# A spectral mixing layer with a snake feed-forward: the first batch's stage on pairs of PSUM banks, its filter in three groups, with copies moved to GpSimd

## The chip, the core and the metric

The kernel runs on one core of a Trainium2 chip. The metric is the device time of one launch in microseconds. Names of engines in the profile: PE is TensorE's matmul and PEld its weight load, DVE is VectorE, ACT is ScalarE, POOL is GpSimd, SP is SyncE, which only issues DMAs here.

## The reference

```python
X = np.fft.rfft(x, axis=1)                     # x: 8 x 3008 x 256
y = np.fft.irfft(X * (filt_r + 1j * filt_i), n=3008, axis=1)
h = y.reshape(24064, 256) @ w_in               # 256 x 2048
g = h + np.sin(alpha * h) ** 2 / (alpha + 1e-9)
out = g @ w_out                                # 2048 x 256, float32
```

## The kernel before, in words

The sequence of 3008 points is taken as 47 x 64, so that both transforms become matmuls with small tables: a first stage over 47, a turn of the data, a stage over 64 in 24 classes of frequencies, a product with the filter, and the same back. Weights are folded: `w_in` is multiplied by alpha, `w_out` by -1/(2 alpha), and the loop then needs only a cosine.

Most of the time is a loop of 48 chunks of up to 512 columns: `hidden` (the first product, line 601, cosine on ACT at L605, one operation on DVE at L606) and `project` (the second product, L621). The transforms of batches 1 to 7 are put between its steps by a list of places (`put`). PE is nearly always busy there.

Before the loop can begin stands the head: the transform of batch 0, done whole in SBUF, and the loads and folding of weights. The order on every engine is the order of the program text (a manual schedule). The head's steps, with the names that the change and the prediction touch:

- Loads. SP loads the first quarter of x in two halves (into `cos_all`). POOL's queue loads the other three quarters, the table `d_t`, an identity `id16`, and then the filter: for each of two groups of 12 classes, two DMAs of the real part, two of the imaginary part, and one for `e_t` (L364, L368). At most eight of POOL's DMAs are under way: each further one waits on POOL for the landing of the one eight before it. `split_alpha` on POOL splits alpha in three bf16 parts between those issues. SP's `w_in` DMAs wait for the landing of the real part of group 1; small tables and `w_out` are queued behind them on SP.
- Stage one. `warm_pe` runs matmuls on a zero tile, so as to keep PE busy. `cast_x0` casts the first quarter of x in two halves on DVE; between them DVE takes the reciprocal of alpha on 16 partitions (L455). 16 matmuls `pa` (L459), each into a PSUM bank of its own out of the pools `hps` (4 banks) and `fps` (2), evacuated on DVE and ACT in turn into `t1_0` (L185 and L187, the helper `evac`).
- `spread_alpha` (L353, L355) broadcasts alpha over partitions by matmuls and copies by ACT, one bank at a time, twice early and twice at the head's end. `inverse_table` (L426, L428) makes `e1_0` from `d_t`.
- `turn` (L473) turns blocks of 32 on DVE: four to get `t2_0`, and two of twice the size (`turn_back`) at the end.
- `other_half` completes the filter on 128 partitions: a copy of the real part to partitions 64 to 127 (L187) and a negation of the imaginary part to partitions 0 to 63 (L445), both on DVE, per group of 12.
- 12 blocks of 4 classes and half of the channels: `forward_0` (PE `pb` L491, ACT L495), `product_0` (DVE, L501, real and imaginary part in one instruction), `inverse_0` (PE `pc` L513, ACT L185).
- `reciprocals` turns 1/alpha to 128 partitions through PE. Then 12 warming matmuls and `last_0` (PE `pd` L403), which give the first columns of `y`, on which `hidden` works.
- `weights_in` and `weights_out` on POOL (L542, L574) fold alpha in. The first waits for the last product.

Of the kernel before, what the change touches and what calls it, by code (L numbers as in the profile page):

```python
# [9 lines left out]
FP16 = mybir.dt.float16  # L10
# [12 lines left out]
NR = 2 * N1  # L23
# [48 lines left out]
def kernel(  # L72
# [31 lines left out]
    def pool(name, bufs, space=None):  # L104
        kw = {} if space is None else {"space": space}
        return ctx.enter_context(tc.tile_pool(name=name, bufs=bufs, **kw))
# [4 lines left out]
    xfpool = pool("xf", 3)  # L111
    ppool = pool("pp", 7)
    xspool = pool("xs", 3)
# [4 lines left out]
    fps = pool("fps", 2, PSUM)  # L118
    hps = pool("hps", 4, PSUM)
    ops = pool("ops", 2, PSUM)  # L120
# [203 lines left out]
    al, rest, rec = [w2_cols[0:16, 256 * i:256 * i + 256].bitcast(FP32) for i in range(3)]  # L324
# [23 lines left out]
    def spread_alpha(i):  # L348

        ps = hps.tile([128, 4, 128], FP32, name=f"al_bc_{i}", tag="h")  # L350
        for a in range(4):
            for k, part in enumerate(parts):
                nc.tensor.matmul(out=ps[:, a, :], lhsT=one[:, 4 * i + a:4 * i + a + 1].to_broadcast([128, 128]),  # L353
                                 rhs=part, start=(k == 0), stop=(k == 2))
        nc.scalar.copy(out=alpha[:, i // 2, 512 * (i % 2):512 * (i % 2) + 512], in_=ps.rearrange("p a b -> p (a b)"))  # L355

    for g in range(2):
        gs = slice(12 * g, 12 * g + 12)
        for k, filt in enumerate((filt_r, filt_i)):
            for q in range(2):  # L360
                if (g, k, q) == (0, 1, 1):
                    split_alpha()
                off, step = ((12 * g) * C, C) if q == 0 else ((N1 - 12 * g) * C, -C)
                marks["filt", g, k] = nc.gpsimd.dma_start(  # L364
                    out=f_t[k][64 * k + 32 * q:64 * k + 32 * q + 32, gs, :],
                    in_=bass.AP(tensor=filt.tensor, offset=filt.offset + off,
                                ap=[[N1 * C, 32], [step, 12], [1, C]]))
        nc.gpsimd.dma_start(out=e_t[:, gs, :], in_=e_dram.ap()[:, gs])  # L368

# [23 lines left out]
    def last_0(n0, n, own=fps, tag="f", spread=False):  # L393

        for cb in range(2):
            made = []

            def one(i, cb=cb, made=made):

                if i == 0:  # L400
                    ps = own.tile([128, 512], FP32, name=f"pd_0_{n0}_{cb}", tag=tag)
                    made.append(ps[:, 0:n * NR].rearrange("p (a r) -> p a r", r=NR))
                nc.tensor.matmul(out=made[0][:, i, :], lhsT=t4_cols[:, n0 + i, :, cb], rhs=wi0_t,  # L403
                                 start=True, stop=True)
                if i == n - 1:
                    evac(y[:, cb, 0, n0:n0 + n, :], made[0], cb == 0)

            for i in range(n):
                if spread:
                    between.append(lambda i=i, one=one: one(i))  # L410
                else:
                    one(i)

    def reciprocals():

        ps = ops.tile([128, 512], FP32, name="ps_rec", tag="o")
        nc.tensor.transpose(out=ps[:, 0:16], in_=rec, identity=id32)
        nc.vector.tensor_scalar(out=rec_t, in0=ps[:, 0:16], scalar1=-0.5, scalar2=None, op0=ALU.mult)

    def inverse_table(g):  # L420

        gs = slice(8 * g, 8 * g + 8)
        ps = ops.tile([128, 8, 128], FP16, name=f"pse_{g}", tag="o")
        for i in range(8):
            for a in range(2):
                nc.tensor.transpose(out=ps[64 * a:64 * a + 64, i, :],  # L426
                                    in_=d_t[:, 8 * g + i, 64 - 64 * a:128 - 64 * a], identity=id16)
        nc.scalar.mul(e1_0[:, gs, :], ps, -0.125)  # L428

    warmed = []  # L430

    def warm_pe(n):

        warmed.append(n)
        ps = hps.tile([128, 512], FP32, name=f"warm_{len(warmed)}", tag="h")
        for i in range(n):
            nc.tensor.matmul(out=ps, lhsT=idle[:, 0:128], rhs=idle[:, 0:512], start=True, stop=True)  # L437

    def other_half(g, k, on_act):

        gs = slice(12 * g, 12 * g + 12)
        if k == 0:
            evac(f_t[0][64:128, gs, :], f_t[0][0:64, gs, :], on_act)
        else:
            nc.vector.tensor_scalar(out=f_t[1][0:64, gs, :], in0=f_t[1][64:128, gs, :],  # L445
                                    scalar1=-1.0, scalar2=None, op0=ALU.mult)
# [8 lines left out]
    nc.vector.reciprocal(out=rec, in_=al)  # L455
    for i in range(16):
        own, tag = (fps, "f") if i % 3 == 2 else (hps, "h")
        ps = own.tile([128, 512], FP32, name=f"pa_0_{i}", tag=tag)
        nc.tensor.matmul(out=ps, lhsT=wf0_t[0:NR], rhs=x0[i // 4][:, 2 * (i % 4):2 * (i % 4) + 2, :],  # L459
                         start=True, stop=True)  # L460
        evac(t1_0[:, 2 * i:2 * i + 2], ps.rearrange("p (n k c) -> p n c k", n=2, k=2), i % 2)
        if i == 1:
            warm_pe(3)
            cast_x0(1)
        if i < 15 and i % 4 == 3:
            warm_pe((2, 2, 2, 1)[i // 4])
    spread_alpha(0)
    spread_alpha(1)
    warm_pe((2, 2, 2, 1)[3])
# [10 lines left out]
    for i in range(4):  # L480
        turn(t2_0[i // 2][:, :, 32 * (i % 2):32 * (i % 2) + 32], t1_0[:, :, 32 * i:32 * i + 32])
        if i > 1:
            other_half(0, i - 2, False)
    blocks = [(hc, w) for hc in range(2) for w in range(3)] + [(0, 3), (1, 3), (0, 4), (0, 5), (1, 4), (1, 5)]
    xf0, p0 = {}, {}

    def forward_0(i):
        hc, w = blocks[i]
        ps = hps.tile([128, 4, 128], FP32, name=f"pb_0_{i}", tag="h")
        for j in range(4):  # L490
            nc.tensor.matmul(out=ps[:, j, :], lhsT=d_t[:, 4 * w + j, :],  # L491
                             rhs=t2_0[hc][:, 4 * w + j], start=True, stop=True)
        own, tag = (xspool, "xs") if i % 2 else (xfpool, "xf")
        xf0[i] = own.tile([128, 4, 128], FP16, name=f"xf_0_{i}", tag=tag)
        nc.scalar.copy(out=xf0[i].rearrange("p s (k c) -> p s k c", k=2),  # L495
                       in_=ps.rearrange("p s (c k) -> p s k c", k=2))

    def product_0(i):
        hc, w = blocks[i]
        p0[i] = xpool.tile([128, 2, 4, 128], FP16, name=f"p_0_{i}", tag="x")  # L500
        marks["products"] = nc.vector.tensor_tensor(  # L501
            out=p0[i].rearrange("p f s (k c) -> p f s k c", k=2),
            in0=xf0[i].rearrange("p s (k c) -> p s k c", k=2)[:, None].to_broadcast([128, 2, 4, 2, 64]),
            in1=filt_t[:, :, 4 * w:4 * w + 4].rearrange("p f s (k c) -> p f s k c", k=2)[..., 64 * hc:64 * hc + 64],
            op=ALU.mult)

    def inverse_0(i):
        hc, w = blocks[i]
        ps = fps.tile([128, 4, 128], FP32, name=f"pc_0_{i}", tag="f")
        for j in range(4):  # L510
            s = 4 * w + j
            for k in range(2):
                nc.tensor.matmul(out=ps[:, j, :], rhs=p0[i][:, k, j, :],  # L513
                                 lhsT=e_t[:, s, :] if k == 0 else e1_0[:, s, :],
                                 start=(k == 0), stop=(k == 1))
        evac(g_0[hc][:, 4 * w:4 * w + 4], ps.rearrange("p s (k c) -> p s c k", k=2), not (i in ()))
# [4 lines left out]
    for g in range(6):  # L521
# [5 lines left out]
        if g == 0:  # L527
            after(ins, marks["filt", 1, 0])
# [19 lines left out]
    [inverse_table(g) for g in range(2)]  # L548
    for i in range(6):
        forward_0(i)  # L550
        if i % 3 == 2:
            if i == 2: inverse_table(2)
            warm_pe((4, 0)[i // 3])
    for i in range(13):
        for e in {5: [(1,0,False)],6: [(1,1,False)]}.get(i, ()):
            other_half(*e)
        if i < 12:
            product_0(i)
        if i == 11:
            reciprocals()  # L560
        if i > 0:
            inverse_0(i - 1)
        if i + 6 < 12:
            forward_0(i + 6)
        if i == 12:
            turn_back(0)
    turn_back(1)

# [8 lines left out]
    spread_alpha(2)  # L577
    spread_alpha(3)
# [6 lines left out]
    last_0(4, 2, hps, "h")  # L585
# [113 lines left out]
    for n0, n, at in ((6, 5, 1.5), (11, 4, 11), (15, 4, 13), (19, 4, 15.5), (23, 4, 17), (27, 5, 19)):  # L699
        put(at, last_0, n0, n, fps, "f", True)  # L700
# [91 lines left out]
```

## Time and profile before

| | |
|---|---|
| median of three runs | 776.99 us (776.43 to 777.83) |
| profiled execution, its own time | 779.76 us |
| its span, first to last instruction | 778.0 us |
| mean granted TensorE clock | 0.997 |
| first `hidden` matmul (chain) | 38.70 us |

The profiled execution is one run with the hardware profiler on; its own time is a little above that of the runs without it. The page gives busy times by engine (part 1) and the chain of work that ended last (part 4). The chain of waits lists the same chain in order of time: start in us, length, engine, tile and line. A timeline lists instructions of an engine in order, merged (x2 is two of them), with the idle time before and what ended it. A view of busy times by stretch adds PE's granted clock, where 1.00 is full speed.

### The profile page before, as it was taken

To read this page: it belongs to the slowest core of one execution; us is meant where nothing else is said; L and a number is where in the kernel's file an instruction comes from. 1 tells how busy PE (TensorE), PEld (TensorE's weight loads), DVE (VectorE), ACT (ScalarE), POOL (GpSimd) and SP (SyncE) were. 2 spreads that over 40 slices of the span, in tenths; PEclk is the share of its full clock that TensorE was granted. 3 is DMA by queue.
4 is the path that set the end of the run, shared out by engine and by line. 5 is a ranking of instruction groups with operands and counts; after the bars stand their busy time and mean duration, and the time that the engine had idled before them with its cause. 6 is when DMAs were issued, how large, how long until landed. Compare 5 with 4: busy or idle time off the path is not lost.

```text
span 778.0 us, 17230 instructions
## 1 busy us (share of the span) xinstructions
PE 764.5 (98%) x6039; PEld 517.0 (66%) x6039; DVE 658.0 (85%) x1174; ACT 610.4 (78%) x1204; POOL 370.4 (48%) x649
## 2 busy tenths in 40 slices
PE   7999999999999999999999999999999999999997
PEld 3757766666666666666666666766666666766665
DVE  6986998999988888898889988898888888787773
ACT  5798888898878877888878787788778787777762
POOL 6355555634555655455464647554454645430000
PEclk9999999999999999999999999999999999999999
DMA  9955578864765428644474536864254322511112
GB/s 223 267 108 160 119 181 242 220 137 124 187 165 133 124 58 219 154 108 127 107 194 121 139 95 145 198 152 120 72 145 110 87 70 56 135 46 34 37 41 56
DMA packets 81518, 101.49 MB, mean 130 GB/s; under 512 B 18884, under 2 KB 60864, under 8 KB 81431
## 3 DMA queue, kind: packets, MB, share of 16 engines
q0 software_dynamic: 27440, 47.29, 26.1%
q1 hardware_dynamic: 53434, 52.79, 25.4%
q8 instruction: 47, 0.77, 0.4%
q10 hardware_dynamic: 557, 0.31, 0.2%
q14 instruction: 40, 0.33, 0.1%
HBM read 56.15 MB, written 46.66 MB: 132 GB/s over the span
## 4 chain that ended last, share of the span: by engine, by line
PE 91%; DVE 5%; ACT 1%; issue 1%; DMA 1%; ACTq 0%; DVEq 0%
PE po L621 40%; PE ph L601 40%; DVE v L606 3%; PE pd L316 2%; PE pb L243 2%; PE pa L222 2%; PE pc L293 1%; ACT cos_all L605 1%; PE pc L513 1%; DMA w<-in_moe_alpha_dram 1%; PE warm L437 1%; PE pb L491 1%; PE pa L459 1%; PE pa L206 0%; PE pd L403 0%
## 5 line engine op out<-in xcount | busy, mean ns | idle before, releaser
L606 DVE SCALAR_TENSOR_TENSOR v<-cos_all,ph 128x512 f16<-128x512 f32 (+1 forms) x768 | 482.5, 671 | 99.2 <-ACT cos_all L605 95.7
L605 ACT ACTIVATE cos_all<-ph 128x512 f32<-128x512 f32 (+1 forms) x768 | 413.9, 600 | 101.8 <-PE ph L601 98.5
L665 POOL DMA_DIRECT2D out_dram<-o x530 | 291.7, 557 | 244.1 <-ACT o L630 215.3
L621 PE MATMUL po<-w,v 128*128 128x256 f16 x3008 | 389.9, 273 | 0.9 <-DVE v L606 0.9
L601 PE MATMUL ph<-y,w 128*128 128x512 f16 (+1 forms) x1536 | 389.1, 375 | 1.3 <-DVE v L606 1.1
L621 PEld LDWEIGHTS <-v 128*128 128x128 f16 x3008 | 289.9, 98 | 85.9 <-DVE v L606 1.5
L601 PEld LDWEIGHTS <-w 128*128 128x128 f16 x1536 | 143.1, 98 | 114.0 <-issue 19.1
L630 ACT COPY o<-po 128x512 f32<-128x512 f32 (+1 forms) x95 | 56.1, 591 | 7.6 <-PE po L621 6.9
L246 ACT CAST xf<-pb 128x512 f16<-128x512 f32 x84 | 51.1, 608 | 2.0 <-PE pb L243 1.2
L185 ACT CAST y<-pd 128x376 f16<-128x376 f32 (+1 forms) x86 | 42.1, 491 | 12.3 <-PE pd L316 8.8
L160 POOL DMA_DIRECT2D x<-in_x_dram x48 | 25.6, 538 | 40.1 <-DVE v L606 26.8
L185 ACT CAST t_h<-pa 128x512 f16<-128x512 f32 (+1 forms) x60 | 32.8, 590 | 12.5 <-PE pa L222 11.3
L316 PEld LDWEIGHTS <-t_a 96*128 96x128 f16 x448 | 31.4, 97 | 12.7
L264 DVE TENSOR_TENSOR p<-p,xs 128x512 f16<-128x512 f16 x84 | 35.7, 425 | 2.9
L263 DVE TENSOR_TENSOR xs<-xs,filt_t 128x512 f16<-128x512 f16 x84 | 35.1, 418 | 1.6 <-DMA xs<-xf 1.6
L257 DVE TENSOR_TENSOR p<-xf,filt_t 128x512 f16<-128x512 f16 x84 | 35.0, 417 | 0.0
L185 ACT CAST gt<-pc 128x512 f16<-128x512 f32 x54 | 28.1, 595 | 8.4 <-PE pc L293 8.4
L187 DVE CAST t_h<-pa 128x512 f16<-128x512 f32 (+1 forms) x52 | 33.5, 682 | 0.2
L243 PE MATMUL pb<-t,d_t 128*128 128x256 f16 x168 | 32.1, 273 | 0.6 <-ACT cos_all L605 0.6
L316 PE MATMUL pd<-wh_t,t_a 96*128 96x94 f16 x384 | 31.8, 204 | 0.0
L235 POOL DMA_DIRECT2D t<-d x28 | 24.4, 874 | 12.0 <-DMA d<-t_h 10.9
L243 PEld LDWEIGHTS <-d_t 128*128 128x128 f16 x168 | 16.3, 98 | 15.1 <-DMA t<-d 0.8
(70 smaller groups left out, 278.0 us busy)
## 6 DMA issues: line engine op xcount, KB each, us to landing
t<-d POOLq DMA_DIRECT2D x28, 384.0 KB, 5.2
xs<-xf SPq DMA_DIRECT2D x168, 64.0 KB
t_a<-d SPq DMA_DIRECT2D x28, 384.0 KB
x<-in_x_dram POOLq DMA_DIRECT2D x50, 188.0 KB, 4.5
d<-t_h SPq DMA_DIRECT2D x48, 192.0 KB
d<-gt SPq DMA_DIRECT2D x36, 256.0 KB
out_dram<-o POOLq DMA_DIRECT2D x91, 64.0 KB, 2.1
out_dram<-o POOLq DMA_DIRECT2D x31, 80.0 KB, 3.6
```

The source lines that it names most:

```text
L185: marks["act"] = nc.scalar.copy(out=dst, in_=src)
L243: nc.tensor.matmul(out=ps[:, i, :], lhsT=d_t[:, s, :], rhs=self.t2[s // 6][:, s % 6, :], start=True, stop=True)
L246: nc.scalar.copy(out=self.xf[u], in_=ps)
L263: nc.vector.tensor_tensor(out=xs, in0=xs, in1=f_t[1][:, 2 * u:2 * u + 2, :], op=ALU.mult)
L264: nc.vector.tensor_tensor(out=p, in0=p, in1=xs, op=ALU.add)
L316: nc.tensor.matmul(out=psv[:, i, :], rhs=wi_t if self.b < TILED else wh_t, start=True, stop=True, lhsT=t4_h[ch // 2][0:NK, n0 % 16 + i, cb ...
L601: nc.tensor.matmul(out=ps[:, 0:n], lhsT=w1[:, cb, jb * 128:jb * 128 + 128], rhs=y_cols[:, cb, c0:c0 + n], start=(cb == 0), stop=(cb == 1))
L605: nc.scalar.activation(out=cs[:, 0:n], in_=ps[:, 0:n], func=AFT.Sin, bias=float(np.pi / 2))
L606: marks["snake"] = nc.vector.scalar_tensor_tensor(out=v[k][:, jb, 0:n], in0=cs[:, 0:n], scalar=-1.0, in1=ps[:, 0:n], op0=ALU.add, op1=ALU. ...
L621: nc.tensor.matmul(out=pso[k][:, t % 2, :], lhsT=v[k][:, jb, 128 * t:128 * t + 128], rhs=w2[:, jb, :], start=(jb == 0), stop=(jb == 15))
L630: copy(out=o[:, i0:t % 2 + 1, :], in_=pso[k][:, i0:t % 2 + 1, :])
L665: queues[i % len(queues)].dma_start(out=bass.AP(tensor=out.tensor, offset=out.offset + t0 * C, ap=[*ap, [1, C]]), in_=o_blk[p0:p0 + rows, :])
```

## The change

It touches the head alone.

- The PSUM pools are opened only after the head. In the head one block of eight banks, `banks`, stands in their place: three pairs of banks are dealt in turn (`two_banks`), bank 6 is for `inverse_table` and `reciprocals`, bank 7 for warming matmuls. `spread_alpha`, `forward_0` and `inverse_0` now work on a pair of banks, with one evacuation of 1024 columns.
- The filter and `e_t` are loaded in three groups of 8 classes, so 15 DMAs and not 10. `w_in` waits for the imaginary part of the third group.
- The real part is copied to the other partitions by POOL (`real_half`), as 32-bit words; the first of three copies stands in POOL's queue behind the DMAs of the second group and ahead of those of the third, the others behind them.
- The blocks are 6, of 8 classes and half of the channels, in an order written out by hand; real and imaginary products are separate instructions. The evacuation of one inverse block is divided between ACT and DVE.
- Alpha is turned to 128 partitions first, early in stage one, and its reciprocal taken there.
- Both early evacuations of stage one go to ACT; the counts of warming matmuls differ; half of alpha is spread early and half at the head's end.

```diff
+    head = ctx.enter_context(ExitStack())
+    work = pool("work", 6, ctx=head)
+    banks = pool("banks", 1, PSUM, ctx=head).tile([128, 8, 512], FP32, name="banks")
+    def two_banks():
+        turns[0] += 1
+        at = 2 * (turns[0] % 3)
+        return banks[:, at:at + 2].rearrange("p b c -> p (b c)")
...
-    for g in range(2):
-        gs = slice(12 * g, 12 * g + 12)
+    def real_half(g):
+        gs = slice(8 * g, 8 * g + 8)
+        nc.gpsimd.tensor_copy(out=f_t[0][64:128, gs].rearrange("p s c -> p (s c)").bitcast(UINT32),
+                              in_=f_t[0][0:64, gs].rearrange("p s c -> p (s c)").bitcast(UINT32))
+
+    for g in range(3):
+        gs = slice(8 * g, 8 * g + 8)
...
         nc.gpsimd.dma_start(out=e_t[:, gs, :], in_=e_dram.ap()[:, gs])
+        if g == 1:
+            real_half(0)
+    real_half(1)
+    real_half(2)
...
     def reciprocals():
-        ps = ops.tile([128, 512], FP32, name="ps_rec", tag="o")
-        nc.tensor.transpose(out=ps[:, 0:16], in_=rec, identity=id32)
-        nc.vector.tensor_scalar(out=rec_t, in0=ps[:, 0:16], scalar1=-0.5, scalar2=None, op0=ALU.mult)
+        ps = banks[:, 6]
+        nc.tensor.transpose(out=ps[:, 0:16], in_=al, identity=id32)
+        nc.vector.reciprocal(out=rec_t, in_=ps[:, 0:16])
+        nc.vector.tensor_scalar(out=rec_t, in0=rec_t, scalar1=-0.5, scalar2=None, op0=ALU.mult)
...
     cast_x0(0)
-    nc.vector.reciprocal(out=rec, in_=al)
     for i in range(16):
-        own, tag = (fps, "f") if i % 3 == 2 else (hps, "h")
-        ps = own.tile([128, 512], FP32, name=f"pa_0_{i}", tag=tag)
+        if i % 2 == 0:
+            ps = two_banks().rearrange("p (a c) -> p a c", c=512)
...
-        evac(t1_0[:, 2 * i:2 * i + 2], ps.rearrange("p (n k c) -> p n c k", n=2, k=2), i % 2)
+        evac(t1_0[:, 2 * i:2 * i + 2], ps[:, i % 2].rearrange("p (n k c) -> p n c k", n=2, k=2), i < 2 or i % 2)
         if i == 1:
-            warm_pe(3)
+            warm_pe(5)
             cast_x0(1)
+        if i == 3:
+            reciprocals()
         if i < 15 and i % 4 == 3:
-            warm_pe((2, 2, 2, 1)[i // 4])
+            warm_pe((2, 4, 2)[i // 4])
     spread_alpha(0)
-    spread_alpha(1)
-    warm_pe((2, 2, 2, 1)[3])
...
+        parts = ((0, 4, True), (4, 4, False)) if (hc, g) == (0, 2) else ((0, 8, True),)
+        for j, n, on_act in parts:
+            evac(g_0[hc][:, 8 * g + j:8 * g + j + n], ps[:, j:j + n].rearrange("p s (k c) -> p s c k", k=2), on_act)
...
         if g == 0:
-            after(ins, marks["filt", 1, 0])
+            after(ins, marks["filt", 2, 1])
...
+    inverse_table(0)
+    forward_0(0, 0)
+    inverse_table(1)
+    forward_0(0, 1)
+    warm_pe(2)
+    forward_0(1, 0)
+    product_0(0, 0, 0)
+    imaginary_half(0)
+    product_0(0, 0, 1)
+    forward_0(1, 1)
+    inverse_table(2)
+    product_0(1, 0, 0)
+    inverse_0(0, 0)
+    imaginary_half(1)
+    product_0(1, 0, 1)
+    forward_0(0, 2)
+    inverse_0(1, 0)
...
+    imaginary_half(2)
+    for hc in range(2):
+        for f in range(2):
+            product_0(hc, 2, f)
+    for hc in range(2):
+        inverse_0(hc, 2)
+    spread_alpha(1)
+    turn_back(0)
     turn_back(1)
+    head.close()
+    released.append(True)
+    flip[0] = 2
+    xfpool = pool("xf", 3, reuse_waits="tile")
...
-    spread_alpha(2)
-    spread_alpha(3)
```

## The prediction

> **What bounds the kernel now.** I read the page first, its parts 1 and 4: PE is busy almost the whole span and carries nearly the whole chain.
>
> ```profile
> PE 764.5 (98%) x6039; PEld 517.0 (66%) x6039; DVE 658.0 (85%) x1174; ACT 610.4 (78%) x1204; POOL 370.4 (48%) x649
> PE 91%; DVE 5%; ACT 1%; issue 1%; DMA 1%; ACTq 0%; DVEq 0%
> ```
>
> From the last turn back on, both kernels have the same instructions in the same order on each engine, so a time can only come from when that loop starts: the first ph matmul at 38.70 us in the chain. I then read the chain of waits for the first 40 us, which says what sets 38.70.
>
> ```profile
> 6.62 0.94 DVE w L455
> 7.56 0.55 DVE t L187
> 8.11 0.60 DVE x L187
> 8.76 1.01 PE pa L459 x2
> 9.77 0.85 PE warm L437 x2
> ...
> 16.89 1.00 DVE t_a L473
> 18.02 1.20 DVE t L473
> 19.23 0.95 DVE filt_t L187
> 20.20 1.26 DVE t L473
> ...
> 34.38 2.59 PE warm L437 x12
> 36.98 1.28 PE pd L403 x12
> ```
>
> Three stretches. To 15.7 us: the casts and stage one, with the reciprocal of alpha (L455, 0.94) ahead of the second cast of x. From 15.7 to 32.2: DVE. From there to 36.98: turning back on DVE, and 12 warming matmuls on PE that end at the same moment. DVE's timeline shows that the middle stretch is full, real copies (L187, 0.95 each) and negations (L445) between transposes and products:
>
> ```profile
> 15.72 2.37 DVE L473 STREAM_TRANSPOSE t_a<-t 128x1024 uint32<-128x1024 uint32 x2 [0.16 <-ACT t L185]
> 18.02 1.20 DVE L473 STREAM_TRANSPOSE t<-t 128x1024 uint32<-128x1024 uint32 x1
> 19.23 0.95 DVE L187 COPY filt_t<-filt_t 64x3072 f16<-64x3072 f16 x1
> ...
> 28.47 3.70 DVE L501 TENSOR_TENSOR p<-xf,filt_t 128x1024 f16<-128x1024 f16 x6
> ```
>
> Last, busy times by stretch (length, then PE, PEld, DVE, ACT, POOL, PE's granted clock, DMA share, GB/s):
>
> ```profile
> 5.28:8.70 3.42, 1.64 (x7) 0.58 (x6) 2.56 (x4) 0.65 (x1) 1.77 (x3) 1.00 1.07 211
> 8.70:12.11 3.41, 3.35 (x8) 1.13 (x8) 1.56 (x4) 1.22 (x2) 3.12 (x10) 0.50 1.09 303
> 15.52:18.94 3.42, 2.72 (x54) 2.30 (x52) 3.26 (x4) 3.13 (x6) 1.20 (x3) 1.00 1.18 246
> ```
>
> PE waited 1.70 us at L459 for the cast and was 48% busy in the first of these; in the second it had half clock, 0.43 for a 512-column matmul that takes 0.22 elsewhere. DMA is saturated (share over 1), so arrivals are fixed by bytes.
>
> **Stage one.** The reciprocal on 16 partitions (0.94) leaves DVE; the new one works on 128x16, an eighth of the columns, so 0.2 to 0.3 with its scaling of 0.17, after the third and fourth tiles. The first two evacuations go to ACT, idle there (3.75 us before its first). So the second cast follows the first at about 6.5, when that half of x has landed (6.42 in the trace's queue record), and ends near 7.2 instead of 8.71. PE bridges with 5 warming matmuls (5 x 0.22 = 1.1) and stays busy. It then waits only for x: by time to landing these come at 7.9, 9.6, 10.5 and 11.6. After 11.6 there are two matmuls and a backlog of evacuations at 0.5 to 0.65 each per engine; transposes start near 13.2 instead of 15.72, 2.5 earlier. Of that, 8 matmuls x 0.21 = 1.7 is the half clock.
>
> **Middle stretch on DVE.** Before, by rows: four transposes 4.8, twelve products 3.10 + 0.69 + 3.70 = 7.5, two copies 1.9, two negations 1.9; 16.1, and 16.45 with gaps. After: transposes 4.8, products 7.5 (twelve again, 1024 columns each), three negations of 2048 in place of two of 3072. A negation's 0.956 less some 0.15 fixed gives 0.69 each, 2.1. The sum is 14.4: the copies' 1.9 gone, 0.15 added. Two banks to one copy on ACT cost 1.04 (L428, 1024 columns, 1.94 for two) against two of 512 at a pitch of 0.51: nothing gained. On ACT the row is alpha, table, xf, table, xf, xf; with the identity landed at 14.4 the third xf ends near 20.7, while DVE is ready for its product at 19.8. So 0.9 of waiting is added; the last product ends at 13.2 + 14.4 + 0.9, about 28.3 less overlaps, instead of 32.17.
>
> **The copies on POOL.** Three of 64x1024 words stand between filter DMAs. No row shows such a copy. Nearest: POOL's cast of 16x128 takes 0.28 and of 16x16 0.19, 0.8 ns a column, so about 1.0; its two-input product takes 1.85 for 768, 2.4 ns, so 2.5 at most. I take 1.0, since it has one input. The first stands ahead of the five DMAs of the third group (0.56 each, 2.8) and so delays them to 17.7 to 20.5. Their bytes would reach the head of the full queue only near 21.5 (the first two groups are two thirds of what landed by 25.1), so this is hidden; if the queue ran dry it would cost up to 1. Copies end near 17.7, 21.5 and 23.2; products need them at 17.9, 22.6 and 25.7: hidden.
>
> **w_in.** Its issue by SP now waits for the third imaginary filter (about 23.6, instead of 20.97), with wf, wt, wh, wi and w_out behind it on SP. The first three pieces then land by 27 to 29.5; the products on POOL, which wait for the last product of the head, begin at 28.3. Hidden by about a microsecond; its price if late is what exceeds that.
>
> **Tail.** From the last product, T = 28.3: DVE evacuates half a block (0.65; the block's products ended 1.25 earlier), then turns back twice at 2.25, ready at T + 5.2; before it was T + 4.75. On PE: 16 inverse matmuls (0.9), 24 for alpha's second half (1.34), then the 12 warming matmuls, whose buffer now is the two banks that ACT reads alpha from. They wait for a 1.1 us copy, and pd, queued behind them, begins at T + 0.1 + 0.9 + 1.34 + 0.15 + 1.1 + 2.59, T + 6.2. PE is late by 1.0 where DVE was. pd at 34.55.
>
> **Sum.** With the same durations and handovers of 0.06 to 0.25 the order of before comes to 37.66, where the trace has 36.98: the method runs 0.7 long. Like against like, 37.66 to 34.55, 3.1 us. The profiled execution took 779.76 (span 778.00 and 1.76 around it), so its like would take 776.65. The median, 776.99, is 2.8 below, and the three times spread over 1.40 (776.43 to 777.83), nearly the 1.7 of the half clock. I read that as the dip being there in some executions and not in others, and count half of it: 3.1 - 0.85 = 2.25, so 774.7. If all runs had the dip it is 773.9, if none 775.6. The Trainium skill (TensorE: Matmul & The Clock Gate, Part 1) says that the gate's window of 3413 ns is free-running and so varies with the phase at start; the dip here lasts about that long, and by that rule the half is right.
>
> **Rivals.** What this measurement can tell from no change is about 0.2%, 1.55 us.
>
> First, the gate closes elsewhere. PE now waits for the identity near 13.5 to 14.4 and for the transposes to 15.7; a stretch of 3.4 us there is some 63% busy by my sum. Against it: 2.72 of 3.42, 80%, kept the clock. For it: 1.64, 48%, lost it. Half clock there or in stage one costs 1.7: 776.4, no difference. Chance 0.12.
>
> Second, POOL's second and third copies meet DVE's products. Nothing in the trace has POOL computing beside a product (L501). If each held the other up for its length, two times 1.0 falls on DVE, the bound: 776.7. Chance 0.14. The Trainium skill (SBUF — State Buffer, Who interferes with whom) has this rule: a DVE instruction with two SBUF inputs and a GpSimd one that reads SBUF exclude each other, whoever came first. By it the sum would lose between 0 and 2.0; no run here shows it yet. For a small loss: products leave no gap, and POOL's copies have time to spare.
>
> Third, slower: the copy on POOL, which writes 64 partitions away from where it reads, takes c far over 1.0. The copies end at about 16.7 + c, 19.5 + 2c and 19.5 + 3c; the second is needed at 22.6, so from c = 1.55 each microsecond costs 2. At 2.7 the gain of 2.25 is gone, at 3.5 the kernel is 1.65 slower, 778.6. Against: even the two-input rate gives only 2.5, 776.6. Chance 0.13 for a loss.
>
> Fourth, the earlier start is hidden later: w_out and the x of batch 1 come by bytes, not by the head. x of batch 1 landed at 41.6 to 49.2 and was used from 48.2; 3 us sooner still leaves slack. 777.0, chance 0.05.
>
> **Numbers.** My forecast, 774.7, has the remaining 0.56, its own range 773.0 to 776.0. The range 772.8 to 777.6 takes in the first, second and fourth rivals, and the two-input rate of the third. Faster by over 0.2% (below 775.4): the forecast's share of 0.5, and some 0.14 from the weak ends of the rivals, 0.64. Slower: most of the third, and mishaps like it, 0.14. Between: 0.22.
>
> **What would show it.** In the profile after: transposes from near 13; no half clock after 5.3 us; POOL's copies of about 1.0; the last product ending near 28; warming matmuls starting right behind ACT's copy of alpha, and pd 1 us after DVE is ready; first ph near 35.5. I am wrong if products wait for POOL, if a stretch before 20 us has half clock, or if pd waits for DVE.

## The result, and the profile after

| | before | after |
|---|---|---|
| median of 14 runs each | 777.2 us (776.26 to 778.93) | 779.96 us (778.53 to 785.87) |
| ratio | | 1.0051, 95% interval 1.0034 to 1.0069 |
| profiled execution, its own time | 779.76 us | 780.09 us |
| its span | 778.0 us | 778.3 us |

The changed kernel is slower by 0.5%, where a gain of 2.3 us was forecast. Its 14 times fall in two groups: nine from 778.5 to 780.6 and five from 783.2 to 785.9.

Stage one came out as forecast: the transposes start at 13.36, where 13.2 was expected. Busy times by stretch of the profile after, in the columns of those of before (length, then PE, PEld, DVE, ACT, POOL, PE's granted clock, DMA share, GB/s):

```profile
5.28:8.70 3.42, 3.32 (x16) 1.37 (x15) 2.10 (x5) 1.76 (x3) 1.78 (x4) 1.00 1.08 213
8.70:12.11 3.41, 3.41 (x17) 1.54 (x16) 2.91 (x6) 2.42 (x4) 2.98 (x9) 1.00 1.07 300
```

PE is busy in both and the clock is full. But here is the second of these stretches of a kernel that has the program of before with some tiles of the loop at other places in SBUF (`before_addr` below; ratio to before 1.0003, 0.9995 to 1.0012):

```profile
8.70:12.11 3.41, 3.41 (x17) 1.53 (x16) 3.22 (x6) 3.01 (x6) 3.03 (x8) 1.00 1.09 315
```

The order of before has no half clock here either. The profiled execution of before, at 779.76, lay above all 14 of its timed runs: its half clock belongs to that execution. Of four profiles with this same stage one, and three more with the reciprocal moved, only that one shows it. Nor is it the profiler that makes an execution longer, as was supposed above: the profiled execution of `before_addr` took 776.72, less than the median of that kernel's runs, 777.62. Where the disturbance began shows in DVE's rows, first of before and then of `before_addr`:

```profile
6.62 0.94 DVE L455 RECIPROCAL w<-w 16x128 f32<-16x128 f32 x1 [0.86 <-DMA w<-in_moe_alpha_dram]
8.04 0.67 DVE L187 CAST x<-cos_all 94x1024 f16<-94x1024 f32 x1
```
```profile
5.70 0.93 DVE L455 RECIPROCAL w<-w 16x128 f32<-16x128 f32 x1
7.10 0.66 DVE L187 CAST x<-cos_all 94x1024 f16<-94x1024 f32 x1
13.15 2.37 DVE L473 STREAM_TRANSPOSE t_a<-t 128x1024 uint32<-128x1024 uint32 x2 [0.17 <-ACT t L185]
```

Alpha landed late in the execution shown above (why is not known), the reciprocal waited 0.86 for it, the second cast came 0.94 later, PE stood for 1.70, and then came the half clock, another 1.7. Together that is about the 2.57 by which its transposes are late. The head to compare with begins its transposes at 13.15 and its loop at 36.13, not at 15.72 and 38.70.

The timeline of DVE after, from the first transposes on, and of POOL beside it:

```profile
13.36 2.37 DVE L485 STREAM_TRANSPOSE t_a<-t 128x1024 uint32<-128x1024 uint32 x2 [0.16 <-ACT t L190]
...
18.69 1.48 DVE L458 TENSOR_SCALAR filt_t<-filt_t 64x2048 f16<-64x2048 f16 x1
20.20 2.13 DVE L509 TENSOR_TENSOR p<-xf,filt_t 128x1024 f16<-128x1024 f16 x2
22.37 0.69 DVE L458 TENSOR_SCALAR filt_t<-filt_t 64x2048 f16<-64x2048 f16 x1
23.09 3.82 DVE L509 TENSOR_TENSOR p<-xf,filt_t 128x1024 f16<-128x1024 f16 x5
```
```profile
16.49 1.03 POOL L365 COPY filt_t<-filt_t 64x1024 uint32<-64x1024 uint32 x1
...
18.55 1.10 POOL L375 DMA_DIRECT2D filt_t<-in_filt_i_dram  x2
19.61 0.69 POOL L379 DMA_DIRECT2D e_t<-e_tbl  x1
20.29 1.50 POOL L365 COPY filt_t<-filt_t 64x1024 uint32<-64x1024 uint32 x1
22.39 1.58 POOL L365 COPY filt_t<-filt_t 64x1024 uint32<-64x1024 uint32 x1 [0.59 <-DMA filt_t<-in_filt_r_dram]
```

A negation takes 0.69 at 22.37 and 1.48 at 18.69, beside POOL's issues of DMAs. Two products take 2.13 (1.29 elsewhere) and five 3.82 (3.10 before). In the records of single instructions the product of 20.82 ends at 22.34, 0.55 behind the end of POOL's copy (21.79), and that of 23.09 at 24.50, 0.54 behind the next copy (23.96): each ended as if it had run only when the copy was over. The copy that began in a product's time took 1.50, and the one that began in a negation's 1.58, and not 1.03. The first copy, beside transposes, lost nothing. Last, the chain of waits at the end of the head, after, and of the undisturbed order of before:

```profile
31.21 1.35 PE banks L358 x24
...
32.59 1.02 ACT y L360
33.61 0.04 issue
33.65 2.75 PE warm L453 x12
36.40 1.01 PE pd L418 x12
...
37.85 0.50 PE ph L630 x2
```
```profile
30.48 1.34 PE al_bc L353 x24
31.82 2.59 PE warm L437 x12
34.41 1.28 PE pd L403 x12
...
36.13 0.51 PE ph L601 x2
```

The head is 1.72 longer: 0.21 up to the first transpose, 0.36 from there to the last product (30.16 against 29.59), and 1.15 behind it, where PE waits for ACT's copy of alpha (L360). The loop loses 1.20 more at one place, the first `pb` of batch 1 (73.00). There batch 1, after its first stage, is stored to DRAM (`d`, in four stores) and loaded back turned (`t`) for the second. The view of the tile `t` between 60 and 76 us gives the waits of those who read and write it, in us and times:

```profile
its engine sat idle before it (us, times) until:
  DMA d<-t_h: 7.0, 1
  DMA t<-d: 1.0, 1
```

POOL's reload of batch 1 (`t<-d`) waits for the store of `d`, and PE waits 1.03 for the reload (0.00 in the undisturbed profile). The order of before can meet this wait too: its profile shown above lost 0.8 at the same place. 1.72 and 1.20 are 2.9 of the 3.4 between the spans of these two profiles (778.3 and 774.9), and the medians are 2.8 apart. The group above 783 is another matter.

### The profile page after: what moved, and what is told of

Same layout as the page of the kernel before. It is cut to its first block, busy times and chain, and to the rows that moved or that the text cites. A ratio compares the mean times of both kernels' runs of the same rounds, so it can differ in the third digit from the quotient of the medians.

```text
span 778.3 us, 17218 instructions
## 1 busy us (share of the span) xinstructions
PE 763.6 (98%) x6040; PEld 517.4 (66%) x6040; DVE 658.0 (85%) x1173; ACT 609.9 (78%) x1191; POOL 377.1 (48%) x657
## 4 chain that ended last, share of the span: by engine, by line
PE 86%; DVE 6%; DMA 3%; ACT 3%; issue 1%; POOL 0%; ACTq 0%; SPq 0%; DVEq 0%; POOLq 0%
PE po L650 39%; PE ph L630 38%; DVE v L635 4%; PE pd L321 2%; PE pb L248 2%; PE pa L227 2%; DMA xs<-xf 1%; PE pc L298 1%; ACT cos_all L634 1%; DVE p L509 1%; DMA d<-t_h 1%; ACT xf L502 1%; DMA t<-d 1%; DMA cos_all<-in_x_dram 1%; PE pa L211 0%
## 5 line engine op out<-in xcount | busy, mean ns | idle before, releaser
L190 ACT CAST gt<-pc 128x512 f16<-128x512 f32 x54 | 28.1, 594 | 8.4 <-PE pc L298 8.4
```

The source lines that it names most:

```text
L190: marks["act"] = nc.scalar.copy(out=dst, in_=src)
```

## The experiments

**Four theories for the loop and the middle stretch.** The loop's instructions are the same and in the same order, yet the loop is longer, and in a third of the runs by 5 us more. The expectations name the theories A to D.

`lanes`:

```diff
+    tiny = cpool.tile([128, 3], FP32)
+    for i in range(3):
+        nc.gpsimd.dma_start(out=tiny[0:16, i:i + 1], in_=id32_dram.ap()[:, i:i + 1])
```

> The changed kernel with three tiny DMAs more on GpSimd's queue, behind its last copy of the filter: 18 DMAs from the filter on in place of 15, so that the loop's DMAs on that queue fall on the same eight semaphores, in the same turn, as in the kernel before (10 and 18 differ by 8). Theory A (the turn of the queue's eight semaphores is what makes the loop slower: a load or store waits on another predecessor): the loop takes as long as before, 739.3 us from the first hidden matmul to the end, and the time falls to about 776.5. Theory B (the loop starts before its data of batch 1 is there, whatever the semaphores): as the changed kernel, 778.5 to 786.

781.96 (779.83 to 784.46), ratio 1.0063 (1.0045 to 1.0081): theory A falls. Its profile was of a long execution, 784.46, and shows what such a one is. Its waits from 44 to 56 us (engine and line, what ended the wait, us in total, times, longest):

```profile
...
DVE v L638 <- ACT cos_all L637: 3.4, 3, 2.5
ACT w L606 <- DMA w_out<-in_moe_w_out_dram: 2.8, 1, 2.8
PE ph L633 <- DVE v L638: 2.8, 2, 2.2
```

The second half of `w_out`, issued by SP at 31.80, landed at 48.19 (42.48 in the first profile after, 39.17 before). Of that DMA's sixteen completions fifteen had come by 43.16; why the last one was 5 us behind them was not followed. ACT folds it in at the loop's steps 5 to 6.5; it stood there for 2.8, the cosines behind it, DVE behind those, PE 2.2 behind DVE; and then PE had half clock from 50.70 to 54.11. Between 46 and 54.5 us this execution loses 3.7 against the first profile after.

`before_addr`: the three pools `xf`, `pp`, `xs` opened behind `vp`.

> The kernel before with the pools of the loop's xf, p and xs tiles opened behind the pool of v, which puts every tile of the loop at the SBUF addresses that it has in the changed kernel. Theory C (those places make the loop slower): 779 to 786, with the changed kernel's spread. Theories A and B: no difference, 776.3 to 779.

777.62, ratio 1.0003 (0.9995 to 1.0012): theory C falls.

`late_loop`: `warm_pe(12)` becomes `warm_pe(16)`.

> The changed kernel with 16 warming matmuls in place of 12 ahead of the first columns of y: the loop starts 4 x 0.22 = 0.9 us later, about where it started before (38.7). Theory B (data of batch 1 comes at its own time, and an earlier loop runs into it, stalls and loses the clock): nothing is lost by the delay, and the slow cluster of executions (783 to 786) goes; 777 to 779. Rivals A (semaphores) and C (places in SBUF): 0.9 us slower than the changed kernel, 779.4 to 786.8, with the cluster still there.

779.83 (779.23 to 780.58, five runs), first hidden matmul 1.14 later than in the changed kernel. The median is not in theory B's range of 777 to 779. None is above 781, but five runs are few to tell that from luck; the wait at `pb` stayed at 0.49.

`dve_copy`:

```diff
-        nc.gpsimd.tensor_copy(out=f_t[0][64:128, gs]..., in_=f_t[0][0:64, gs]...)
+        nc.vector.tensor_copy(out=f_t[0][64:128, gs], in_=f_t[0][0:64, gs])
```

> The changed kernel with the three real copies on DVE, each right ahead of the first product that needs it, and none on GpSimd. Theory D (GpSimd's copies and DVE's operations on the filter exclude each other, and that is what ate the head's gain): a negation takes 0.69 everywhere (1.48 was seen), the first two products 1.3 (2.13) and the five 3.2 (3.82), 2.2 us less on DVE, against two copies of 0.65 that fall on its path (the first stands where DVE waits for its operand): the last product ends near 29.2 where it ended at 30.16, and the first hidden matmul is 0.9 earlier, 36.9. Rival: the long rows were late operands and not exclusion; then the last product ends 1.3 later, at 31.4.

780.61 (778.63 to 786.85), ratio 1.0051 (1.0031 to 1.0071). The rows shrank as theory D said (negations 0.69, every product pitch 0.60 to 0.62), but the last product ended at 30.47. Three copies cost DVE 2.3 (0.79, 0.73 and 0.79 from one start to the next); on GpSimd they had cost it 2.35. I had hidden the first copy under a wait of DVE for its operand, the third xf. By the records of single instructions that xf ended at 20.75 in the changed kernel and the product that reads it began at 20.82; without the 0.79 more of the negation DVE would have been there at 20.03. So the negation already stood in that wait, and taking it away and putting a copy in its place changes little. No run shows the wait as idle time.

**Is it w_in?** The long executions show `w_out` late, and `w_out` is queued on SP behind `w_in`.

`early_w_in` and `before_late_w_in`, the same edit in both directions:

```diff
-            after(ins, marks["filt", 2, 1])
+            after(ins, marks["filt", 1, 1])
```
```diff
-            after(ins, marks["filt", 1, 0])
+            after(ins, marks["filt", 1, 1])
```

> The changed kernel with one edit: SP's first w_in DMA waits for the imaginary part of the second filter group (landed at 20.20) and not of the third (23.86), so w_in, the small tables, w_out and what follows leave SP some 3.3 us earlier, as in the kernel before (20.97). Theory E (w_in held back three microseconds pushes the second half of w_out to 42 to 48 us, and where it lands after 48 ACT, which folds it in at the loop's steps 5 to 6.5, holds up the cosines, and PE idles and loses the clock): the second half of w_out lands by about 39 to 41, and no execution is above 781; the median falls from 780 to about 778.8, that is, by what the slow third of the executions and the waits for batch 1 added. Rival G (the slow third is something else, such as the clock alone or the head): the third stays, 783 to 786.

> The kernel before with one edit: its first w_in DMA waits for the imaginary part of the second (last) filter group (landed at 23.5 to 24.4) and not for the real part (20.95). Theory E: w_out and the x of batch 1 come some 3 us later, while its loop starts at 36.1, earlier than that of the changed kernel; so it gets the same slow executions and more of them: median 778.5 to 783, highest above 783. Rival G: 776.3 to 779, no difference but what POOL's folding of w_in waits (w_in would land from 28 on, and it begins at 29.7).

The changed kernel with early `w_in`: 780.4 (778.83 to 780.81), none long. Six kernels in which `w_in` leaves SP that early gave 59 runs, the highest 780.81; the changed kernel itself, in 26 runs, gave eight above 782 (the kernel before, with `w_in` as early, gave two in its 135 runs here, both in the last comparison; what made those long is not known). The kernel before with late `w_in`: 780.96 (779.79 to 783.13), ratio 1.005 (1.0034 to 1.0065). This one edit makes the kernel before as slow as the changed one. Its waits from 40 to 56 us:

```profile
...
ACT w L572 <- DMA w_out<-in_moe_w_out_dram: 2.0, 1, 2.0
PE ph L601 <- DVE v L606: 2.0, 2, 1.5
```

Half clock followed, from 49.32 to 52.74. Theory E stands for the long executions: late `w_in` brings them. Two of them were traced to the wait for `w_out`. That the median of `early_w_in` did not fall is the part of the forecast that failed: the typical executions, by the two that were traced (780.09 and 779.15), do not have this wait.

`changed_again`, the changed kernel beside others with early `w_in`:

> The changed kernel as it is, beside the others on this chip. Theory E (late w_in) expects some executions above 782 in it, and none in kernels with an early w_in; the median 779.5 to 781. Rival: on this chip it has none either.

780.82 (778.8 to 788.78), ratio 1.0051 (1.0028 to 1.0074), three of 12 above 782.

**The tail.** `early_w_in_own_bank` takes the warming tile from the pool of the second product; `tail_free` writes the 12 matmuls ahead of `head.close()`, into bank 7.

```diff
     turn_back(1)
+    warm_pe(12)
     head.close()
...
-    warm_pe(12)
     last_0(0, 4)
```

> The same early w_in, and the warming matmuls ahead of the first columns of y in a bank of their own (out of the pool of the second product, idle until then), so that they no longer wait for ACT's copy of alpha (1.10 us of waiting in the changed kernel's trace). Theory E with the tail as it was forecast: first hidden matmul about 0.9 to 1.0 earlier than in the changed kernel, then bound by DVE's turns back, and the time 0.9 below the run with early w_in alone, about 777.9. Rival: the earlier loop runs into batch 1's data and nothing is gained.

> The changed kernel with early w_in, and the 12 warming matmuls ahead of the first columns of y written before the head's PSUM block is given back, into its bank 7, which nothing else uses then. In the run with a bank of the new pools they still waited 1.10 us for ACT's copy of alpha, since tiles of the new pools wait for all work on the old block. Now PE should go on from alpha's matmuls without a gap, be done 1.1 us sooner and end with DVE's turns back: first hidden matmul about 1.0 earlier than with early w_in alone (37.88), 36.9, and 1.0 off the time, 779.2. Rival: the first columns of y wait for the same copy or for DVE, and nothing is gained.

The other bank changed nothing: 1.10 of waiting for ACT as before, 779.23. With `reuse_waits="tile"` the new pools wait for all work on the old block, alpha's copy included. `tail_free`: 778.89 (778.07 to 779.74), ratio 1.0017 (1.0009 to 1.0026). Its chain:

```profile
31.26 4.51 DVE t_a L485 x2
...
35.82 1.28 PE pd L418 x12
...
37.53 0.52 PE ph L630 x2
```

`pd` now comes right behind DVE. The gain in the start of the loop was 0.52 and not 1.0, in a profile with half clock at 24.7 to 28.1. The wait at `pb` was there (0.64), with the reload 4.95 after the store's issue.

**The wait at `pb`.** In the trace's packet records the last store of `d` ahead of it is nearly as quick as ever up to nine tenths (2.4 us behind its issue against 2.3), but in seven profiles of the changed kernel and its kin the last packet ended 3.5 to 4.1 after the issue, where four profiles of the kernel before and its kin have 2.6 to 3.0. In all seven a packet of 16 KB of queue q8, of the kind instruction, began 1.0 to 1.7 us behind the issue, amid the store's. The page of after lists 47 of them:

```profile
q8 instruction: 47, 0.77, 0.4%
```

PE has 12,080 instructions, matmuls and weight loads, 47 times 256 and 48 over, and from one of these packets to the next PE runs about 256 of them; so I take them for fetches of PE's own instructions. Their place in the loop then depends on how many instructions stand ahead of it. `fetch_shift` moves them:

```diff
-            nc.tensor.matmul(out=ps, lhsT=idle[:, 0:128], rhs=idle[:, 0:512], ...)
+            nc.tensor.matmul(out=ps[:, 0:cols], lhsT=idle[:, 0:128], rhs=idle[:, 0:cols], ...)
...
-    warm_pe(12)
+    warm_pe(29, 94)
```

> The changed kernel with early w_in, and 29 warming matmuls of 94 columns (about 29 x 0.09 = 2.6 us) in place of 12 of 512 (2.59 us): 34 PE instructions more ahead of the loop. A block of 256 of them lasts 17 us, so PE's fetches of 16 KB fall some 2.2 us earlier in the loop. Theory F (in the changed kernel such a fetch sits among the packets of batch 1's last d1 store, 1.3 to 1.7 us after its issue, and makes the last packets 1.2 us late, for which pb waits at 73 us): the store takes 3.6 us from issue to the next issue and not 4.6 to 5.2, the gap at pb (0.47 to 1.03 in six profiles) is gone, and the time falls by 0.5 to 0.7, to 779.6. Rival: the late tail of that store has another cause and stays.

778.23 (777.33 to 779.97), ratio 1.001 (1.0001 to 1.002). The fetch came 0.19 behind the store's issue, the reload followed 3.54 later, and the gap at `pb` was gone. The loop also began 0.5 earlier, since the narrow matmuls took 1.4 and not 2.6.

`tail_and_shift`:

> Both: early w_in, 29 narrow warming matmuls in place of 12, written before the PSUM block is given back. Sum of both theories: first hidden matmul near 36.9, no wait at pb of batch 1, 778.6; still about 1 us above the kernel before, for the middle stretch's exclusions (GpSimd against DVE, 2.3) are left in.

779.17 (777.24 to 780.75): no wait at `pb`, yet no faster than either edit alone. Behind narrow matmuls PE lost the clock just as the loop began:

```profile
36.47:39.88 3.41, 3.41 (x11) 1.28 (x11) 1.42 (x3) 1.50 (x4) 3.40 (x4) 0.50 1.00 149
```

`tail_wide`, the same with 29 matmuls of 212 columns:

> The changed kernel with early w_in and 29 warming matmuls of 212 columns ahead of the giving back of the PSUM block: no wait for ACT's copy of alpha, PE busy throughout, no fetch among the d1 store's packets. First hidden matmul near 37.3, no wait at pb, none above 780: 777.9 to 778.3. The rest, 0.7 to 1.0 above the kernel before, is the middle stretch with GpSimd's exclusions. Rival: as with early w_in and wide warming alone, 778.9.

778.03 (777.38 to 778.85), 0.57 above the 777.46 of before in that comparison; ratio 0.9999 (0.9982 to 1.0015), that is, not told from it. First hidden matmul at 37.34, no wait at `pb`, full clock. With late `w_in`, the copy of alpha and the fetch out, what is left of the head is 1.2: 0.2 up to the first transpose, 0.6 in the middle stretch and 0.4 behind the last product, where DVE's half evacuation and turns now set `pd`.

**The middle stretch without any copy.** `dma_copy` (with the narrow matmuls, and `w_in` behind the copies on SP):

```diff
-        nc.gpsimd.tensor_copy(out=f_t[0][64:128, gs]..., in_=f_t[0][0:64, gs]...)
+        nc.sync.dma_start(out=f_t[0][64:128, gs], in_=f_t[0][0:64, gs])
```

> The changed kernel with 29 narrow warming matmuls in place of 12, and the three real copies made by DMAs of SP's queue, each as soon as its real part has landed (15.0, 18.2, 22.3), ahead of w_in on that queue (w_in so leaves SP at 22.3 to 22.6). DVE has no copies then and GpSimd none to exclude it with. Theory D (exclusion by GpSimd took the 1.9 that the copies' leaving DVE was to bring): the last product ends 14.6 to 15 us behind the first transpose, at 28.2 to 28.5 with a start at 13.4, where the changed kernel has 30.16; first hidden matmul near 35.6 and about 776.4. Rival H (DVE is not the bound of the middle stretch: ACT's evacuations or the filter's arrival are): DVE idles ahead of its products, the last one ends at 29.5 or later, and the time is no better than that of the run with narrow matmuls, 778.2.

782.19 (779.65 to 784.55). DVE's timeline:

```profile
20.29 0.69 DVE L505 TENSOR_TENSOR p<-xf,filt_t 128x1024 f16<-128x1024 f16 x1 [1.52 <-DMA filt_t<-in_filt_i_dram]
...
21.74 1.29 DVE L505 TENSOR_TENSOR p<-xf,filt_t 128x1024 f16<-128x1024 f16 x2
...
25.65 2.50 DVE L505 TENSOR_TENSOR p<-xf,filt_t 128x1024 f16<-128x1024 f16 x4 [1.17 <-DMA e_t<-e_tbl]
```

No row is stretched, and less its two waits for DMAs (1.52 and 1.17) the stretch from the first transpose to the last product (14.15 to 31.40) takes 14.6: theory D's size. The wait for the third xf, worked out above, does not show in it, since DVE came to that product late through the first of the two. The copies' bytes stand in the full DMA queues, so the filter itself comes late, rival H's outcome, and `w_out` later still (3.1 of waiting on ACT, two windows of half clock behind it; a third, from 17.68, lies in the head).

**The parts that should help, in the kernel before.** `before_pool_copy`: its first real copy on GpSimd, 64 x 1536 words.

> The kernel before with the first real copy (64 x 1536 words) on GpSimd and the second left on DVE. It runs there from about 16.6 to 18.1, beside DVE's transposes, which the first copy of the changed kernel did not lengthen nor was lengthened by (1.03). Theory D (GpSimd and DVE exclude each other only where DVE runs products, negations and copies): 0.95 leaves DVE's path, less at most 0.2 for the negation behind the last transpose; first hidden matmul at 35.2 to 35.4 where an undisturbed run of the kernel before has 36.13, and about 776.6 against 777.5. Rival: any copy on GpSimd costs DVE as much as it takes; no difference.

777.13, ratio 0.9994 (0.9983 to 1.0004). The loop began 0.22 earlier, not 0.8 to 0.9:

```profile
17.82 1.35 DVE L449 TENSOR_SCALAR filt_t<-filt_t 64x3072 f16<-64x3072 f16 x1
```

The copy ran on POOL from 16.89 to 18.35; the negation that began at 17.82 took 1.35 and not 0.95, having waited for it. DVE's products began 0.6 earlier; the rest was lost at the end, where PE and ACT are late.

`before_two` (also the reciprocals on 128 partitions), `before_two_shift` (29 matmuls of 94 columns) and `before_two_wide` (29 of 212):

> The kernel before with its first real copy on GpSimd and the reciprocals of alpha on 128 partitions early in stage one (with its scaling), as in the changed kernel; nothing else. The first alone brought the first hidden matmul from 36.13 to 35.91. The second takes 0.17 and a wait of 0.19 out of DVE's path ahead of the turns back, and 0.16 of PE's: another 0.2 to 0.3. Expected 776.7 to 777.0 where the kernel before has 777.5; rival: no difference from before, since PE's chain at the end (inverse, alpha, warming) sets pd.

> The kernel before with its first real copy on GpSimd, the reciprocals of alpha on 128 partitions, and 29 narrow warming matmuls in place of 12 (34 PE instructions more ahead of the loop). Without the last edit the loop began 0.47 earlier than in the kernel before, and 1.43 was lost again where pb waits for the d1 store, next to a fetch of PE's instructions. Theory F: that wait goes, 776.2 to 776.7. Rival: the wait stays and the time is that of the kernel before, 777.2.

> As the last of the kernel before (first real copy on GpSimd, reciprocals on 128 partitions), with 29 warming matmuls of 212 columns (29 x 0.09 = 2.6 us) in place of 12 of 512: as many PE instructions as with 29 of 94, but PE busy throughout, which the narrow ones did not keep it (half clock at 35.6 to 39.0). Theory F: the loop begins some 0.45 earlier than in the kernel before, no wait at pb and no half clock, 776.6 to 776.9 where the kernel before has 777.3: the first version below both. Rival: something else takes the 0.45 back, 777.3.

777.28, ratio 0.9996 (0.9987 to 1.0004): the loop began 0.47 earlier and lost 1.43 at `pb`, with the fetch at the very end of the store's packets. 777.67, ratio 1.0013 (1.0 to 1.0027): no wait at `pb`, but half clock from 35.6 to 39.0. 776.81 (776.27 to 779.33) against 777.46, ratio 0.9988 (0.9974 to 1.0003): neither, the loop 0.36 earlier. It is the lowest median of these comparisons, well below the changed kernel, and not told from the kernel before.

## Why the prediction was wrong, point by point

In round numbers the 5.0 between forecast and result are three steps: 1.7 of baseline (the undisturbed head is 2.57 ahead of the one shown, and 0.85 had been taken off), 2.2 in the changed head (3.1 forecast against the one shown, 0.85 measured: 38.70 to 37.85) and 1.2 in the loop.

**Stage one: the baseline.** Forecast 2.5 earlier, transposes near 13.2; they came at 13.36. The step was right against the profile shown and wrong against the runs: the undisturbed order of before starts them at 13.15. The failed step is "I read that as the dip being there in some executions and not in others, and count half of it". None of it should have been counted, nor the rest of the 2.5: it was alpha's late landing in that execution, 0.9, and the half clock, 1.7. The earlier second cast bought nothing. In `before_addr` it ends at 7.76 and in the changed kernel at 7.00, yet the transposes start at 13.15 and 13.36. The term is -0.2 and not +2.5. What gave it away was on the table: the profiled execution stood 2.8 above the median of its own kernel, more than the 1.7 that I gave the dip. The Trainium skill (TensorE: Matmul & The Clock Gate, Part 1) has the window free-running; that its phase varies does not make a dip fall into half of the executions, and here it was in one of four profiles of this stage one.

**Middle stretch: the second rival.** "Durations 14.4" was right without copies (14.6 in `dma_copy`). The third xf came when forecast, at 20.75 (forecast near 20.7). The step that failed is the exclusion, counted at nothing and given 0.14. It took 0.79 on the negation, 0.84 and 0.72 on two products, together 2.35. The 0.79 lay where DVE would have waited for that xf, so it filled most of the 0.9 of waiting that the forecast has; the 1.56 beside the copies came on top, near the rival's "two times 1.0". So the 1.9 that left DVE was spent: the stretch is 0.36 longer than that of the undisturbed order. The Trainium skill (SBUF — State Buffer, Who interferes with whom) states the rule: a lock held for a whole instruction, by whoever comes first. I cited only its line on two SBUF inputs. The same section lists copies and tensor_scalar in their two-port modes, and warns of DMAs that GpSimd issues: there it is they that starve. The 1.35 of `before_pool_copy` agrees. The negation of 1.48 fits the same lock, taken by the issues first; the first negations of `dve_copy` and `dma_copy`, with no issue beside them, took 0.69.

**Copies on POOL.** 1.03 was forecast as 1.0, and holds beside transposes alone. "Products leave no gap, and POOL's copies have time to spare" was the wrong argument: the copies got in between the products all the same, and an engine that leaves no gap is the one that loses when it has to wait.

**w_in.** "Hidden by about a microsecond; its price if late is what exceeds that" asked for one reader only. `w_in` itself landed in time (27.76, first used at 30.40). I had named `w_out` as queued behind it and priced no wait for it; the fourth rival, which touched it, was put at 0.05 and on the side of no loss. Eight of the changed kernel's 26 executions are above 782. By medians the first group of five above 783 is 5.5 above the other nine; in the one long execution traced (`lanes`) the wait and the half clock behind it took 3.7.

**Tail.** The wait for ACT's copy and its size were right: T + 6.1 for `pd`, forecast T + 6.2. T was 30.16 and not 28.3.

**The loop.** I took it as shifted one to one. It lost 1.20 at `pb`, and why is shown by `fetch_shift` and its kin as far as the fetch goes: moving it took the wait away in all six profiles with it ahead of the store's packets. That instruction counts move PE's fetches was on no list of mine.

## What to carry to other kernels

Before a difference is read off one profile, see how its own time stands to the median of the runs: a disturbance that only the profiled execution has is no gain for a change that removes it. Work taken from a bound engine to a neighbour is free only if the two do not exclude each other on that memory, and a load held back must be priced for each tile queued behind it, at the instruction that uses it. Where a change alters the number of instructions ahead of a tight loop, compare the loop at several marks, not its start alone.

## What the runs showed of the hardware

- DVE and GpSimd held each other up as if by whole instructions, also a one-input negation of f16 against a copy (0.95 became 1.35). Beside GpSimd's issues of DMAs (0.49 to 0.65 each elsewhere) the first negation took 1.41 to 1.59 in five of ten profiles with these copies on GpSimd; in the other five it took 0.69 to 0.76 and a product beside it 1.41 to 2.29 (1.50 in `fetch_shift`, with issues alone beside it). The 32 x 32 transposes of words were not held up, nor did they hold up a copy (1.03).
- With a fetch of 16 KB of instructions amid a store of 96 packets the last packet ended 3.5 to 4.1 behind the issue (seven profiles); with the fetch 0.1 to 0.3 behind the issue, ahead of the first packet, 2.6 to 2.9 (six profiles). At the very end of a store it did harm in three profiles (the reload 4.94 after the issue in before, 4.95 in `tail_free`, 5.57 in `before_two`) and little or none in three others (3.57 in `before_addr`). Which it will be, and which DMA engine it falls on, stays open.
- Warming matmuls of 94 columns were followed by half clock as the loop began in two of four kernels (36.47 and 35.60); with 212 columns in as many matmuls there was none in two profiles.
- Open: 0.7 us that the changed kernel's first profile loses between 334 and 366 us against before (`changed_again` does not lose it), and the loop's other differences of 0.3 to 0.5, were not followed.
